# A new written-out order of all engines and loads for fused attention and a two-way maxout layer

## The chip, the cores and the metric

The kernel runs on one core of one Trainium2 chip. The metric is device time in microseconds for one execution; the median of three runs of the kernel before is 359.53 us (359.02, 359.53 and 360.0).

Engines are named as in the profile: PE is TensorE, PEld its weight loads, ACT is ScalarE, DVE is VectorE, POOL is GpSimd, SP is SyncE, which issues most of the DMAs.

## The reference

For 8 batches and 8 heads, with 1152 positions and 64 values per head, neighbouring query rows are averaged in pairs (576 pooled queries), scored against all 1152 keys, put through a softmax, and multiplied by the values. The 4608 resulting tokens of 512 values go through two weight matrices; the larger of the two results goes through a third:

```python
q_pool = q.reshape(B, H, S // 2, 2, D).mean(axis=3)
scores = scale * np.matmul(q_pool, k.transpose(0, 1, 3, 2))
attn = softmax(scores)                       # row maximum taken off first
x = matmul(attn, v).transpose(0, 2, 1, 3).reshape(B * 576, 512)
h1, h2 = x @ w1, x @ w2                      # (512, 1024) each
out = np.maximum(h1, h2) @ w_out             # (1024, 512), float32
```

## The kernel before, in words

**Attention.** Two heads of one batch form a pair; there are 32 pairs. For each pair q, k and v are loaded (0.59 MB each, three buffers for each kind), cast to bf16 by GpSimd (q is summed over its two rows at the same time), and q and k are transposed. For the first five pairs TensorE transposes (`qtrans`, `ktrans_pe`), for the others VectorE transposes q in eight steps (`qtrans_dve`, L446) and a transposing DMA does k (`ktrans`, L436). The scores of all pairs form one long row of 324 groups of 512 columns for both heads. A step `S` (`scores`, L290) computes a group on TensorE in two PSUM banks, with 64-row tiles, both heads at once; a step `E` (`exps`, L305) puts it through the exponential on ScalarE. No maximum is subtracted. Pair i begins in group 10.125 x i; pair 12 in group 121.

**Values.** For each pair and head four chunks of nine matmuls (`chunk`, L569, full 128-row tiles, only 65 columns each) multiply the exponentials with the values and a column of ones. The last 64 queries of two pairs are taken together (`rest`, L584, 18 matmuls each). VectorE divides by the sum; the result is transposed to `xT`, by TensorE (`xtrans_pe`, L660) for eight pairs and by DMA for the others.

**The maxout layer** uses max(h1, h2) = h2 + max(h1 - h2, 0). The difference `wd` of the two weights is formed once by GpSimd (`w_diff`, eight steps, in the order `W_DIFFS`), and the product `w21` of w2 and w_out once by TensorE (`w2t_job` and `w21_job`, L530 and L543). Then `h` jobs (L694) compute the difference for up to 512 tokens and two blocks of 128 features, `p` jobs (L737) the result for 256 tokens, from `xT` with `w21` and from the rectified differences with w_out. Three `z` jobs (L780) do the last 256 tokens. h and p use 64-row tiles, z full ones.

**The order.** Nothing is scheduled at run time. A long string names one step per character, and each character appends the next step of its kind to the program: `S` a score group, `E` an exponential, `A` a chunk or a rest, `0` to `3` one unit (two matmuls) of the h or p job that is open under that number, `4` to `9`, `+` and `-` the emptying of its banks by VectorE or ScalarE, `K`, `Q`, `T`, `W`, `X`, `Z`, `F` other TensorE work (transposes of k and q, of w2, the units of `w21`, transposes to `xT`, the final jobs, filler), `l` a load, `t` and `x` a transposing DMA, `o` and `z` a store, `k`, `q`, `v`, `d`, `e` the steps of GpSimd, `r` a transpose of q on VectorE, and so on. Each engine executes its own steps in the order of the string; `Plan.solve` puts a semaphore wait wherever a step needs what another engine wrote or still reads. `MOE` gives the order of h and p jobs, `BANKS` one digit per job or score group, the PSUM bank it takes, and `LOADS` the order of the loads. From exponential 40 on a load also waits for the exponential two before the latest one in the string (`pace`). The `cost=` numbers are left over from the planner that made the strings and do nothing at run time.

TensorE has 1541 steps with 6009 matmuls, and one weight load for each matmul.

Of the kernel before, what the change touches and what calls it, by code (L numbers as in the profile page):

```python
# [116 lines left out]
def bass_funnel_attn__then__act_maxout2_kernel(  # L117
# [45 lines left out]
    LOADS = (  # L163
# [14 lines left out]
    )  # L178
    MOE = (
        "hhhhpphhhhpphhhhhhhhpphhhhpphhhhphhhhpphhhhphhhhphhhhpphhhhhphhhhphhh"  # L180
    )
    BANKS = (
        "0102346702674670602456042760460245602456012456214624160246246021460234064032646203460426704064036206"
        "2402642604264206250624024624624620742064064060560640640240260246124064024026412640240240240240246246"
        "2562462464267024602462062402462562624640646246246246246206206036026206260202612602402614262642042040"
        "4040645064064062416240204620642642674264240246240634062062462074206406406065060460240240240240202404"
        "2064306426046060467046064060640265026404024024012640260420460142604206406406420101420002406206204232"
    )

    ctx = ExitStack()  # L190
    with ctx:
# [603 lines left out]
        def store_z(lo, c0, c1, o):  # L795
            todo = []
            for half in range(2):
# [91 lines left out]
                 "m": ("Z", 0), "4": ("0", 0), "5": ("1", 0), "6": ("2", 0), "7": ("3", 0),  # L889
                 "8": ("0", 1), "9": ("1", 1), "+": ("2", 1), "-": ("3", 1)}  # L890
        for c in (
            "lululllfyFKklQfgFbKSgklKEKgSgSEFlFSyFFEQblESkSSElKcKElgTEkgShSESlKyEgQlEKbvgSSESlScEAeAlAEcAAAEASlaa"
            "qAESaSaTlEcTSEAlhQqEhSTlEbXvShESjlQcESEAlESbAcAEAlASkSaEaWaSalWaEWaWcAESSlAcAEAKWlEdaSaWWgEWSldiSEXS"
            "jWEkWjlWWWEWqSSlEKWgWWeiEQlSbSEkWWSlEWWvtWWEWSiSvAEKAgKdEAgAlSaSaEqAAAEAlSaEaAEArSdlrSEArAArdESrSWrA"
            "EWrdAAalEAaaXaSdaAaESljWWaEdWaSrWlEWWkSi1E1SlXqtEjS1j1SEv1rS1r1E1reA5AEASlkAErS0a0aE0vt0rSSr0E0qSr00"
            "ErA4AqlAEASa1aE1Slr11xrES11r1kE1ErSA5AEtASrSEArAArESaSaAklaEAaaAaAESr0vl0a0aE0rSxS0rE00r11xr1E0rS114"
            "E1tS11E1rSe1r1E1SrSv1lE11S1Eq11l111ES1r1SElr1A5AEAAlSaSaoEArAoArEASr0q0Ea0a0Srx0ESr0kSr00ElrS0tr0v0E"
            "0rS0r0EArkArEAArSr0lE0S000ESAlAEAaSa0aE0alSaaAAEASal0akE0tXSj0eE1j14S11ESq11o1ESo11qr1E151S1E1Sl1rS1"
            "ErAvA5AlESAErSSlakAaEAtrAArE00Ea0aS0rxES0r00r0E1q4S11E1S1r1vEl1rS1SrEA5lAvEAArSSlErSArAEArAlaAaAEaSa"
            "1a1taE1Sa1a1vE1rSx1r1SEr1e1r1x1ESrS1r1E1qrS1rl1E1AAkEAAlSa1aE1SS1l1EAAAEAlSa1aE1tSr0E050E0Sx00E0rSSr"  # L900
            "0oE0rSo0r0oE0rAoArkEArAAAvSalSaEAaaAaAaEAlSav0a0E0S11110klE0111S10Et5010S1110ESe1111050E011114Sq1111"
            "ElXA5SoSqjESoAjrAAErAAaAalEAr0000Sa0a01E01lr0S1x4E1SrS1r1E1tr1005E00SE0E0rS0r0q1E14S1l1EAkrASrSlEvAr"
            "ArAEArAlaSa1EaSaAaAalAErSv1a1Ea10lrS0x5E0q0S00ESrx11kr0E0rS1t14Ee1S11E1rSS1rE1rAlArEAArS1aqaE1lS1S1E"
            "S11l1E11S1ErtAkArAEArSa1aE11rxS1r0E005S0E0S0ro0SEr0oS0ro0E0qoAAESAkAEAASav0aESaAaaAaAElASalv0aE0SXrt"
            "E0j0S0jrSE1e1r110rE1Sr11l1Er0S500E011lrS11ErS11q11ElA5AASSlEAAaAaEAASa0aE1k0xS411E1SE111t1rESA5AEvoA"
            "rSoSrEAArAEAr0aSa00alE0aSa0a00E0rSlA4AEA0vaSa0lE0rSxSr0k0E0r00rx0EqSr10r0E0trSe10rE0Sr01rE11Sq0E0l0S"
            "00E0S0l0E014S1E11l1SoSEAoAAokEAAaAaAASa1aE1tSrSE1r1E1rSx11rE1Sr11rE11rS1Er1A5qAEAASoSvESoAAAElaAkaAa"
            "AaEla00a0v0Sa00aE1111xS11rE111115100x111e4S01E0005St0000ErS0400E0Sr00rESl0r00r0E00rSlSrE0Sq000ESl000"
            "EAAlAEAAaAaAASaSakE0t0r00Er1E0r1xS14E1S111EroS1r1o1E151S1E1Sr1S1ErA5AvEAAArSklSESAlrAqAEtaaAaAa0aE0a"
            "Sv0a0aESrxSe0r0E01r0x1rE114S1E1S1l1rSE5AAAElASrSEaAaAlArEAqSa1a1E1lSSxr1E1Sr11rE1t1rSk1rE11Sr1E1r11r"  # L910
            "AEAvS1E1SAqlAEAlS1E1SAAlEaSaaAaAEaAaSka1aE1Sx1r1vSE0500x0E0eSr0SErAtArAEArSao0aE00orSSr0EArAAEqASla0"
            "aE0Sx11110E1111S50E00l1Sk11Er1tSE0r1111Er00S50E01r111Sr11E11rSl0500ES4AAEvASroSESroAAqlAEAaAaAaEAlaa"
            "0Sav00E0aSa000t0r1E1k41S1E1rxSe0r00E0rSx1r00E0rS1r01E14lS11E1rSS1lqE1AAEAAAaAaAASa0a0E00xS00E00S411t"
            "Ek11ESr00E0r0Sr10E0r00Sr1E14S111ErSA5AEvAASroSESroAAoAEaAoaAaAaEaSav111aE1a00xS0Er0S1r11xE1rSe0500E0"
            "tS0r0E0r0SrSE0rS0r00E0000E0SS0E00A4EAAAAaAoaAoASaSaE11x11SES11E1E11511E1S11ES11151E11S1E1S1S1EA5AvEA"
            "AAAAaAaAaAaaSaSE0a0a00xSES000E0x0400E0e00SSE00000E0SS0E0000ES0S0E0S00E00040E00S00EoS0oAEAoAAoAaAaAAA"
            "aAaAxAAAAaAaAaAaa0a100a0a30X0j3100j22221330223323020+130-111301313913000233330-2281122000o01111o2911"
            "0101003381133223311339222-2000222022110222330003382232233+221111o111o31-2o1123333222133233+111-11111"
            "111Z9ZZZZZoZZoZZZZZZmZZZZzzZZZZZZZZZZmZZZZZZZzZzmzz"
        ):  # L920
            step(c)
        plan.solve()
# [51 lines left out]
```

## Time and profile before

| what | value |
|---|---|
| median of three runs | 359.53 us |
| the profiled execution: its time, its span | 360.63 us, 358.9 us |
| granted TensorE clock | 1.00 |
| TensorE busy | 349.2 us, 97% |
| ScalarE busy | 315.3 us, 88% |
| VectorE, GpSimd busy | 236.0 us, 143.4 us |
| DMA | 84.67 MB, 236 GB/s on the mean |
| exponentials (L305) | 303.8 us in 336 instructions |

A busy TensorE says that some matmul was on its way, not that it ran at its peak: matmuls overlap, and most rows give one matmul's own duration, several times the distance from one start to the next. The distance between starts in the timeline is the cost of a step. "issue" as a releaser is time in which an engine waited for nothing that the profile shows. The queue "q8 instruction" brings instructions.

### The profile page before, as it was taken

Reading aid. Unit: us, or ns where it says so; the run is one execution under the profiler, and the core shown is the slowest. Engines: PE = TensorE matmul, PEld = TensorE weight load, DVE = VectorE, ACT = ScalarE, POOL = GpSimd, SP = SyncE. Lnnn points to the kernel's source line nnn. Section 1 sums busy time; section 2 is a strip of 40 time slices with the busy share of each in tenths; the row PEclk is TensorE's granted clock in tenths of the full one; section 3 lists DMA queues with packets and bytes.
Section 4 is the critical chain, followed back from the end, with each engine's and each line's share of the span. In section 5 each row is a group of like instructions: output and inputs, shape, how many; then the busy total and the mean of one; then the engine's idle time right before and its main releaser. Section 6 shows DMA issues by size and latency. Waiting matters only on the chain.

```text
span 358.9 us, 13458 instructions
## 1 busy us (share of the span) xinstructions
PE 349.2 (97%) x6009; PEld 218.0 (61%) x6009; DVE 236.0 (66%) x516; ACT 315.3 (88%) x355; POOL 143.4 (40%) x128
## 2 busy tenths in 40 slices
PE   7699999999999999999999999999999999999996
PEld 5465655655566675656664675666676655657663
DVE  3686578977798658976796776884787774514001
ACT  5999989999999989999999898999999898890431
POOL 2446997363645171744417152535425220100000
PEclk9999999999999999999999999999999999999999
DMA  8999999999999999998999989899999853002224
GB/s 264 409 392 395 316 374 257 298 244 291 314 244 315 288 294 297 329 260 148 343 209 301 233 217 305 187 274 255 196 265 228 170 113 75 17 23 59 60 60 117
DMA packets 77434, 84.67 MB, mean 236 GB/s; under 512 B 49216, under 2 KB 50496, under 8 KB 77376
## 3 DMA queue, kind: packets, MB, share of 16 engines
q1 hardware_dynamic: 76592, 83.28, 88.3%
q8 instruction: 47, 0.77, 0.9%
q10 hardware_dynamic: 784, 0.52, 0.5%
q14 instruction: 11, 0.09, 0.1%
HBM read 62.91 MB, written 9.44 MB: 202 GB/s over the span
## 4 chain that ended last, share of the span: by engine, by line
PE 92%; DMA 3%; ACT 2%; SPq 1%; issue 1%; DVE 0%
PE ps L737 25%; PE ps L290 21%; PE ps L569 21%; PE ps L694 18%; PE ps L584 3%; DMA qraw<-in_q_dram 3%; ACT et L305 2%; PE ps L543 2%; PE ps L780 1%; PE ps L660 1%; SPq L325 0%; PE ps L491 0%; PE ps L512 0%; SPq L336 0%; PE ps L663 0%
## 5 line engine op out<-in xcount | busy, mean ns | idle before, releaser
L305 ACT ACTIVATE et<-ps 128x1024 bf16<-128x1024 f32 (+1 forms) x336 | 303.8, 1016 | 14.0 <-PE ps L290 13.1
L290 PE MATMUL ps<-qpT,kT 64*128 64x256 bf16 (+7 forms) x1162 | 114.5, 283 | 1.2 <-DVE qpT L498 0.6
L446 DVE STREAM_TRANSPOSE qpT<-qp 32x288 bf16<-32x288 bf16 x216 | 101.4, 469 | 12.7 <-PE ps L290 6.0
L694 PE MATMUL ps<-xT,wd 64*128 64x512 bf16 (+3 forms) x832 | 84.1, 311 | 0.0
L569 PEld LDWEIGHTS ps<-vE,et 128*128 128x128 bf16 x2304 | 73.6, 97 | 16.9 <-issue 10.0
L569 PE MATMUL ps<-vE,et 128*128 128x65 bf16 x2304 | 81.5, 193 | 1.9 <-issue 1.4
L737 PE MATMUL ps<-wo,stage 64*128 64x512 bf16 x544 | 78.4, 376 | 0.0
L290 PEld LDWEIGHTS ps<-qpT,kT 64*128 64x128 bf16 x1162 | 47.6, 94 | 48.4 <-ACT et L305 15.1
L411 POOL TENSOR_TENSOR qp<-qraw 128x576 bf16<-128x576 f32 x30 | 42.1, 1406 | 53.8 <-DVE qpT L446 48.9
L417 POOL TENSOR_SCALAR vE<-vraw 128x1152 bf16<-128x1152 f32 x32 | 36.9, 1152 | 56.8 <-PE ps L584 39.3
L694 PEld LDWEIGHTS ps<-xT,wd 64*128 64x128 bf16 x832 | 36.0, 94 | 24.5 <-ACT et L305 1.7
L381 POOL TENSOR_SCALAR kbf<-kraw 128x1152 bf16<-128x1152 f32 x31 | 35.7, 1151 | 32.5 <-DMA kraw<-in_k_dram 24.6
L705 DVE TENSOR_SCALAR stage<-ps 128x1024 bf16<-128x1024 f32 (+3 forms) x40 | 39.1, 979 | 13.4 <-PE ps L694 12.7
L737 PE MATMUL ps<-w,xT 64*128 64x512 bf16 x272 | 39.9, 377 | 0.0
L737 PEld LDWEIGHTS ps<-wo,stage 64*128 64x128 bf16 x544 | 25.8, 94 | 18.5
L598 DVE RECIPROCAL rc<-ps 128x4 f32<-128x4 f32 (+1 forms) x64 | 11.8, 184 | 35.5 <-PE ps L569 34.9
L606 DVE TENSOR_TENSOR xnat<-ps,rc 128x256 bf16<-128x256 f32 x64 | 27.2, 424 | 1.9
L429 POOL TENSOR_SCALAR rem<-et 128x1152 bf16<-128x1152 bf16 x16 | 18.4, 1152 | 20.9 <-ACT et L305 20.8
L743 DVE COPY stage<-ps 128x1024 f32<-128x1024 f32 x14 | 17.0, 1216 | 11.6 <-PE ps L737 11.4
L709 ACT ACTIVATE stage<-ps 128x512 bf16<-128x512 f32 (+1 forms) x12 | 6.0, 525 | 17.4 <-PE ps L694 17.4
L785 DVE COPY stage<-ps 128x512 f32<-128x512 f32 (+1 forms) x2 | 1.0, 492 | 25.7 <-PE ps L780 25.7
L737 PEld LDWEIGHTS ps<-w,xT 64*128 64x128 bf16 x272 | 12.6, 94 | 8.5 <-ACT et L305 0.2
(46 smaller groups left out, 138.5 us busy)
## 6 DMA issues: line engine op xcount, KB each, us to landing
vraw<-in_v_dram SPq DMA_DIRECT2D x32, 576.0 KB, 6.1
kraw<-in_k_dram SPq DMA_DIRECT2D x31, 576.0 KB, 7.0
qraw<-in_q_dram SPq DMA_DIRECT2D x31, 576.0 KB, 6.2
out_dram<-stage SPq DMA_DIRECT2D x24, 256.0 KB, 3.8
out_dram<-stage SPq DMA_DIRECT2D x21, 128.0 KB, 3.0
xT<-in_moe_w_dram SPq DMA_DIRECT2D x4, 512.0 KB, 11.2
stage<-in_moe_w_out_dram SPq DMA_DIRECT2D x4, 512.0 KB, 13.6
stage<-in_moe_w_dram SPq DMA_DIRECT2D x4, 512.0 KB, 14.0
```

The source lines that it names most:

```text
L290: last = e.matmul(ps[:, h, col:col + hi - lo], kT[i % 3][rows(h), t, :], qpT[i % 3][rows(h), lo:hi], start=True, stop=True)
L305: op("ACT", lambda e: e.activation(et2[:, :, c:c + z - a], ps[:, :, a - g * W:z - g * W], EXP, scale=scale), r=[f"b{m}", f"b{m + 1}"], w=w ...
L381: op("POOL", lambda g: g.tensor_scalar(kbf[s][:, :, :, :].rearrange("p t h d -> p h t d"), kraw[r][:, :, :, :], 1.0, 1.0, ALU.mult, ALU.mu ...
L411: op("POOL", lambda g: g.tensor_tensor(qpf[s][:, :, :], qraw[r][:, :, 0, :], qraw[r][:, :, 1, :], ALU.add), r=[f"qraw{r}"], w=[f"qp{s}.0", ...
L417: op("POOL", lambda g: g.tensor_scalar(vE[r][:, :, :, 0:D].rearrange("p t h d -> p h t d"), vraw[r][:, :, :, :], 1.0, 1.0, ALU.mult, ALU.m ...
L429: op("POOL", lambda g: g.tensor_scalar(rem[:, :, :, :], src, 1.0, 1.0, ALU.mult, ALU.mult), r=[f"et{i % 2}.{g - first(i)}" for g in range( ...
L446: op("DVE", lambda e: e.transpose(view[dst:dst + 32, :, 32 * pb:32 * pb + 32], qpf[s][src:src + 32, :, 32 * db:32 * db + 32]), r=[f"qp{s}. ...
L569: last = e.matmul(fb[m][:, sb * 66:sb * 66 + 65], et[:, a:a + P], vE[vs][:, t, half, 0:65], start=(t == 0), stop=(t == NT - 1))
L606: todo.append(evac_op("DVE", lambda e, m: e.tensor_tensor(xnat[xs][:, i % NHP, :, half * D:half * D + D], a(m)[:, 0:NCH, 0:D], rc[half][:, ...
L694: last = e.matmul(fb[m + k][:, 0:size], wd[z, ct, (f0 + k) * P:(f0 + k + 1) * P], xT[z, ct, n0:n1], start=(turn == 0 and ct == 0), stop=(t ...
L705: return e.tensor_scalar_max(gT[:, f0:f0 + 2, g0:g0 + size], wide[m // 2][:, :, 0:size], 0.0)
L737: last = e.matmul(fb[m + k][:, :], lhs, rhs, start=(turn == 0 and j == 0), stop=(turn == 1 and j == NC_ + NF - 1))
```

## The change

The kernel's steps and formulas stay, and so do `MOE` and the numbers of loads, jobs and steps. Four strings and lists are replaced: `W_DIFFS` (the order of the eight `w_diff` steps), `LOADS` from its 20th entry to where it becomes regular near pair 17, `BANKS`, and the string of the order. A constant `FOUR = 1` is added that nothing reads. The two order strings have the same 2751 characters in another sequence. They differ most in the first 50 us, less in the middle, and again at the end, where the last h jobs and the last p job are interleaved in another way. The start of each changed part:

```diff
-    W_DIFFS = ((0, 0), (0, 1), (3, 1), (1, 1), (1, 0), (3, 0), (2, 1), (2, 0))
+    W_DIFFS = ((1, 1), (1, 0), (0, 0), (3, 0), (3, 1), (0, 1), (2, 1), (2, 0))
...
+    FOUR = 1
...
-        ("q", 2), ("w", 0, 3), ("q", 3), ("v", 1), ("w", 2, 0), ("w", 2, 1), ("k", 3), ("w", 2, 2),
-        ("w", 2, 3), ("w", 1, 0), ("k", 4), ("q", 4), ("k", 5), ("v", 2), ("v", 3), ("w", 1, 3),
-        ("q", 5), ("w", 1, 1), ("w", 1, 2), ("k", 6), ("q", 6), ("v", 4), ("k", 7), ("v", 5), ("q", 7),
-        ("q", 8), ("k", 8), ("k", 9), ("v", 6), ("v", 7), ("q", 9), ("q", 10), ("k", 10), ("v", 8),
-        ("k", 11), ("k", 12), ("q", 11), ("q", 12), ("k", 13), ("v", 9), ("q", 13), ("v", 10), ("v", 11),
-        ("v", 12), ("v", 13), ("q", 14), ("k", 14), ("v", 14), ("v", 15), ("k", 15), ("k", 16),
+        ("q", 2), ("w", 0, 3), ("q", 3), ("v", 1), ("w", 2, 0), ("w", 2, 1), ("w", 2, 2), ("w", 2, 3),
+        ("k", 3), ("v", 2), ("k", 4), ("q", 4), ("w", 1, 1), ("w", 1, 0), ("k", 5), ("v", 3), ("q", 5),
+        ("w", 1, 3), ("q", 6), ("w", 1, 2), ("k", 6), ("v", 4), ("q", 7), ("k", 7), ("q", 8), ("v", 5),
+        ("k", 8), ("q", 9), ("v", 6), ("q", 10), ("k", 9), ("k", 10), ("k", 11), ("v", 7), ("v", 8),
+        ("v", 9), ("v", 10), ("q", 11), ("v", 11), ("v", 12), ("q", 12), ("q", 13), ("v", 13), ("k", 12),
+        ("v", 14), ("k", 13), ("q", 14), ("k", 14), ("k", 15), ("q", 15), ("k", 16), ("q", 16),
...
-        "0102346702674670602456042760460245602456012456214624160246246021460234064032646203460426704064036206"
+        "0102346540241601204627067462062401627426402316403643064206340436204620432604260345624064206524062402"
...
-            "lululllfyFKklQfgFbKSgklKEKgSgSEFlFSyFFEQblESkSSElKcKElgTEkgShSESlKyEgQlEKbvgSSESlScEAeAlAEcAAAEASlaa"
-            "qAESaSaTlEcTSEAlhQqEhSTlEbXvShESjlQcESEAlESbAcAEAlASkSaEaWaSalWaEWaWcAESSlAcAEAKWlEdaSaWWgEWSldiSEXS"
-            "jWEkWjlWWWEWqSSlEKWgWWeiEQlSbSEkWWSlEWWvtWWEWSiSvAEKAgKdEAgAlSaSaEqAAAEAlSaEaAEArSdlrSEArAArdESrSWrA"
+            "lululllfyFKklFfgQFbFkSlKEKKggSgSlEFySFEQblkESSESlKcESlgTkEShKElgKySEgQlEKbvgSSESlScEAeAlAcEAATElaSaq"
+            "ThESAlhAEScAESlSqaTEaAhlQEvQbSblESScXESElAjAEcAAElSAaaESaSaaAlaAEcSAEWWlWkaWaEWScSlKEvKWgWEWlgSkiSE"
+            "WWWlESqWWKEWgWlSeSESAlWdEAiAAESaldSaAEQSbklAEAAESvataSWEWWqWWWEWWSidSlEKXrEAgEAdljSSjErAXrAdAEjArSSE"
...
```

More of the change, by code (lines that the diff above doesn't have):

```diff
@@ new lines, in bass_funnel_attn__then__act_maxout2_kernel @@
+            "SSE5AAAElArSSaEAaArlAAEr0E0aSa0lE0r1Sxr01Er1S0q0E014S1E1Sq11rSEA5AvEAArSSElSrkArAAErAlAaatAEaSav1a1a"
+            "E11aSa11ErxSeSr11Er11x1r1ESrS1r1E1r1lSr1kE1rAArAElArSta1aE1S1S1EAAAEASa1aE1lS50Ex0q0E0S0SEo00rk0o0Er"
+            "0oSr0o0ESrtArAEvrAArAArSSakEaAaAalAaEAaSav0a0El0S11110E01S11l10E50tS01111E0Se11110E50011114S1111qEXA"
+            "l5SSojESkAjorAAErAAaqAaEAr0000lSa0a001E1rxS01r1ES411r1ESrl1005tE00SE0E0rS0r01E14S11EAlrAvSrSEArAlrAE"
+            "ArAqaSa1EaSlaAaAaAErSv1la1Ea1Srx00E500kS0xE00rS1r0E1etS411E1S1qrSE1rAArEAkArlSa1aE11rS1r1lESS11E1Sl1"
@@ new lines, in bass_funnel_attn__then__act_maxout2_kernel @@
+            "1EAAAEAlSa1aE1t1rS1r1ESr1x01rE005qS0E0S0roAEkAroSr0oE0rSvo000ESlAAEAASla0aESaAaaAaAElASav0aE0SXlrE0j"
+            "tS00jrSE1e1r110rE1Srq111Er0S500lEk011rS11ErSl1111EqA5AAlSSEAAaAalEAASa0aE10xSk411E1SE111t1rESA5AEvoA"
+            "rSoSrEAArAEArSa0a0E0a0aSal0a0E00rSA4EAlASva0aE00rxS0r0kE0SSxr0E0q0r00rE0tSr1e0Er00Sr0E0r0Sr00E0qSl00"
+            "E0S411El1S11EoSAoAEAoAAaAaAlASaSaE11tr11kr1E1rSESx1rE1Sr11rE11rS1Er11Sl11E1Aq5AEAASovSESoAAAElaAaAaA"
+            "aEa00av00lSa00aE1111xSk11rE111115100x111e4S10E0005St0000ErS0400E0SrS0rE00r0l0r0E00rSSrE0lSq000ES00l0"
@@ new lines, in bass_funnel_attn__then__act_maxout2_kernel @@
+            "EAAAEAlAaAaAASa0akESt0r10Er0E0r1xS14E1S111EroS1r1o1E151S1E11rS1SErA5AvEAAArSklSESArtAqAEaaAaAa0aESa0"
+            "v0a0aESrxSe0r0E00r1x14E11S1E1lrS11rSE5AlAAEASrSElaAaAArEASa1la1E1xSSr1E1Srq1t1rE11r11rE1kSr11E1rSSr1"
+            "1ElAAvE1SAEAqlAS1E1SlAAEaSaaAaAElaAaSva1aE1Sx1r1SkE0500x0E0eSr0SErAtArAEArSao0aE00orS0rSEArAAEqASa0a"
+            "E0lS111x10E1111S50E010Sk10lEr11EStr011Er110S50E01r111Sr11E11rS050l0ES4AAEvASroSESroAAqAElAaAaAaEAaa0"
+            "0alv00Sa1aE0000xS41k1E1Sr00xEr00e1rS00rE0t00r0004S1E000rS1rE11rSl11Eq10S41E1l1S1SEAAAEAAaAaAASa0a0E0"
```

45 lines of the change are left out of this document (16 added, 29 removed), and 12 rows, old and new, of the table LOADS.

## The prediction

> **What bounds the kernel now.** I read the page first, then the waits, the windows and the timeline. Busy shares, slices and the chain of the kernel before:
>
> ```profile
> span 358.9 us, 13458 instructions
> PE 349.2 (97%) x6009; PEld 218.0 (61%) x6009; DVE 236.0 (66%) x516; ACT 315.3 (88%) x355; POOL 143.4 (40%) x128
> ...
> PE   7699999999999999999999999999999999999996
> ...
> ACT  5999989999999989999999898999999898890431
> ...
> PE 92%; DMA 3%; ACT 2%; SPq 1%; issue 1%; DVE 0%
> ```
>
> TensorE carries 92% of the chain and is idle for 358.9 - 349.2 = 9.7 us. The changed kernel has the same 1541 TensorE steps and 6009 matmuls, so it can win only idle time, or the cost of one step following another. How the other engine that matters, ScalarE, stands beside it, by stage (columns: stretch, its length, busy and instructions of PE, PEld, DVE, ACT, POOL, then clock, DMA share, GB/s):
>
> ```profile
> 0.00:15.00 15.00, 11.04 (x155) 7.95 (x155) 6.80 (x16) 10.79 (x13) 4.10 (x13) 1.00 0.90 322
> 15.00:47.00 32.00, 30.80 (x577) 19.51 (x575) 23.15 (x47) 31.88 (x37) 22.42 (x19) 1.00 1.08 368
> 49.00:118.00 69.00, 69.00 (x1157) 40.92 (x1155) 56.60 (x126) 67.75 (x76) 38.87 (x33) 1.00 1.11 285
> 118.00:322.00 204.00, 203.48 (x3578) 126.61 (x3576) 143.42 (x310) 192.49 (x214) 76.02 (x63) 1.00 0.90 220
> ```
>
> Four stages. To 15 us TensorE lacks 4.0 us, with DMA at 0.90. From 15 to 118 us both engines are full: ScalarE lacks 0.1 us in the first part and 1.25 us in the second. From 118 us only TensorE is full; ScalarE lacks 11.5 us. Soon after 322 us ScalarE has no exponentials left. The waits of the whole run (us, times, longest) and the two long holes on TensorE:
>
> ```profile
> PEld ps L290 <- ACT et L305: 15.1, 61, 0.4
> ...
> ACT et L305 <- PE ps L290: 13.1, 20, 1.8
> ...
> PEld ps L569 <- issue: 10.0, 37, 1.2
> ...
> PE ps L569 <- issue: 1.4, 2, 0.9
> ```
> ```profile
> 46.92 0.39 PE L543 MATMUL ps<-wo,xT 128*128 128x512 bf16 x1
> 48.19 0.43 PE L569 MATMUL ps<-vE,et 128*128 128x65 bf16 x9 [0.87 <-issue]
> ```
> ```profile
> 135.34 0.76 PE L569 MATMUL ps<-vE,et 128*128 128x65 bf16 x20
> 136.62 0.77 PE L569 MATMUL ps<-vE,et 128*128 128x65 bf16 x20 [0.52 <-issue]
> ```
>
> "issue" means that no semaphore or DMA explains the hole. Most of the 37 on PEld are about 0.2 us, before a change of tile form, which is costed below; two such waits are on PE itself. Where do they fall in the instruction stream?
>
> ```profile
> 0.00:46.93 46.93, 41.77 (x729) 27.39 (x729) 29.89 (x61) 42.60 (x49) 26.45 (x32) 1.00 1.02 353
> 42.10:46.93 4.83, 4.83 (x129) 3.55 (x125) 3.49 (x10) 4.80 (x7) 4.69 (x5) 1.00 1.33 199
> ...
> 0.00:136.10 136.10, 130.07 (x2259) 81.23 (x2260) 99.04 (x218) 129.45 (x145) 75.80 (x72) 1.00 1.07 310
> 129.45:136.10 6.65, 6.65 (x130) 4.43 (x125) 3.79 (x9) 6.24 (x8) 4.84 (x4) 1.00 1.19 266
> ```
> ```profile
> q8 instruction: 47, 0.77, 0.9%
> ```
>
> 729 and 2259 matmuls stand ahead of the holes: 1530 between them, with as many weight loads 3060 instructions. Queue 8 moved 0.77 MB in 47 packets, 16.4 KB each; 0.77 MB over 12,018 matmuls and loads is 64 bytes an instruction, so a packet is some 256 of them, and 3060 is twelve packets less about one wait instruction in each. Both holes lie on a packet's edge: TensorE had run out of fetched instructions.
>
> **The change, part by part.**
>
> *The fetch at 48 us.* The single L543 matmul at 46.92 should take 0.22 us (six of them take 1.40 us in the chain below), and the next starts 1.27 us later: the hole costs 1.05 us. The packet ahead of it (128 matmuls) began near 42.0 us and ran dry in 4.9 us, while the next packet was there only 6.2 us after that start. In the new order I count matmuls 602 to 729: 46 in L569 against 67, 8 in L543 against 1, 14 transposes against none, the rest equal. An L569 matmul costs 0.030 us (20 from 135.34 to about 135.95), a transpose some 0.06 (four, with a change of tile form, from 328.21 to 328.54).
>
> ```profile
> 34.03 1.40 PE ps L543 x6
> ```
> ```profile
> 328.21 0.40 PE L660 MATMUL ps<-ident,xnat 128*128 128x128 bf16 x4
> 328.54 0.20 PE L663 MATMUL ps<-ident,xend 64*128 64x64 bf16 x1
> ```
>
> So the packet lasts 4.9 - 21 x 0.030 + 7 x 0.22 + 14 x 0.06 = 6.6 us, over the 6.2. At 136 us the packet began at 129.3 and its successor came 7.3 us later. With 6.2 nothing is left of the hole, with 7.3 still 0.7. I take 6.2, the nearer in place and traffic: **-1.05**, ends -0.35 and -1.05. ScalarE gains it too, since its hole there is as long:
>
> ```profile
> 45.41 3.78 ACT L305 ACTIVATE et<-ps 128x1024 bf16<-128x1024 f32 x4
> 50.24 3.88 ACT L305 ACTIVATE et<-ps 128x1024 bf16<-128x1024 f32 x4 [1.05 <-PE ps L290]
> ```
>
> The Trainium skill speaks against this term. Its page "Runtime: NRT & Kernel Launch", section "Instruction fetch mechanics", has the sequencer fetch the next 16 KiB block of 256 instructions while it runs the current one, and calls the cost of a boundary "mostly hidden". The trace agrees on the block's size, and on most of its 47 edges; on two it doesn't. By the rule alone this term and the next would be 0.
>
> *The fetch at 136 us.* Twenty L569 matmuls from 135.34 end near 135.95; the hole to 136.62 is 0.67 us. The 128 matmuls ahead are the same in the new order (18 of p, 40 of h, 24 scores, 6 transposes, 40 of L569), so it is filled only if the packet comes sooner. The loads in front differ: v15 is moved from after exponential 117 to after 134, and k16 from after 120 to after 129, behind q15. That packets can come in time for shorter stretches, two windows show:
>
> ```profile
> 65.00:70.00 5.00, 5.00 (x125) 3.71 (x120) 4.75 (x14) 5.00 (x7) 2.05 (x2) 1.00 1.19 244
> ...
> 124.60:129.30 4.70, 4.70 (x136) 3.83 (x132) 3.06 (x10) 4.05 (x5) 3.13 (x4) 1.00 0.88 219
> ```
>
> Packets of 5 us there cost no hole. Between -0.67 (gone) and +0.67 (twice as long), with one or two loads fewer queued in front: **-0.3**.
>
> *Changes of tile form.* Two h pairs followed by scores take 0.44 us, two followed by L569 0.53 us:
>
> ```profile
> 59.54 0.59 PE L694 MATMUL ps<-xT,wd 64*128 64x512 bf16 x4
> 59.98 0.38 PE L290 MATMUL ps<-qpT,kT 64*128 64x256 bf16 x4
> 60.19 0.59 PE L694 MATMUL ps<-xT,wd 64*128 64x512 bf16 x4
> 60.72 0.75 PE L569 MATMUL ps<-vE,et 128*128 128x65 bf16 x19
> ```
>
> 0.09 us for going from 64-row tiles to the full array. Counted in the two order strings, the old one has 203 neighbours of unlike tiles, the new one 199: 4 x 0.09 = 0.36 at most. All four are saved by the score step 92, near 93 us, where ScalarE paces and TensorE would only wait longer for it. I take **-0.1**, ends -0.36 and 0.
>
> *Score steps placed earlier.* In the ScalarE-paced stage the new order puts some score steps ahead of other work, S96 by 1.8 us, onto a bank that exponential 93 frees, S94 by 0.5. The bank can't be free sooner, since ScalarE has no slack. Other such waits are at most 0.4 us each (the first waits row). While ScalarE paces they cost nothing at the end; as far as it doesn't, they add. **+0.15**, ends 0 and +0.8.
>
> *Start and loads.* The first 19 loads keep their order, and with them the 4.0 us that TensorE lacks. Then the four loads of w_out go together, two of them now ahead of k3, and three of w1 behind k4 and q4. k3's row:
>
> ```profile
> L325 SPq DMA_DIRECT2D kraw<-in_k_dram x1: 4710/4710/4710, 11.6 to 11.6; - x1
> ...
> DMA to landing us min/median/max: 15.8/15.8/15.8
> ```
>
> It lands at 27.4; two 0.52 MB loads at 398 GB/s (the next row) put it at 30.0, its cast (L381, 1.15 us) ends at 31.2, and by equal TensorE work its transposes come at 31.5. Cost 0, cover 0.3 us; without the cover TensorE waits that much longer, behind it the scores of pair 3. GpSimd's w_diff steps follow the arrival of w1 and end at about the same place. 0, ends -0.3 and +0.5.
>
> ```profile
> 15.00:25.00 10.00, 8.83 (x197) 6.37 (x194) 8.38 (x15) 9.91 (x12) 6.27 (x5) 1.00 1.03 398
> ```
>
> *SyncE's queue from 60 to 160 us.* SyncE issues in order, so a load that waits for its ring holds every transposing DMA and store behind it. k9 is issued ten exponentials later, q9 eleven earlier; v9 to v14 come six to eleven earlier, k12 to k16 two to twenty later. The v loads need the cast three pairs back: v12 after exponential 96 has it after 91, v13 after 100 has it after 93, so none should hold the queue. GpSimd's casts (L381, L411, L417) move with their loads; it is busy 38.87 of 69.0 us in that stage and has room. VectorE's eight L446 transposes for each pair end within some 3 us of where they did; pair 9's end six earlier. I cost all this at nothing: the cover is the 2.8 us of pair 12, the tightest, in the third rival.
>
> *Tail.* TensorE has as much work, the last feed-forward jobs are closed in another order, and the three final jobs with their stores are the same: 0. `FOUR` is read nowhere.
>
> Sum: -1.05 - 0.3 - 0.1 + 0.15 = -1.3 us. The profiled execution took 360.63 us, its span and 1.73 us around it: 359.3. The median shown, 359.53, lies 1.1 lower: **358.2**.
>
> **The rivals.**
>
> *Fetch waits only move* (the change doesn't do what it says). Edges stay where the count puts them, and the traffic of the reordered loads delays other packets: for it, one packet at 129 us needed 7.3 us; against it, the 6.6 us packet above. The first two terms fall away: 359.53 - 0.1 + 0.15 = 359.6. The skill's rule of hidden fetches ends there too.
>
> *All of it is won.* Both holes (1.72), all four changes of form (0.36) and 0.3 at the start: 357.1. For it, TensorE has nothing else that waits after 118 us; against it, ScalarE's pace before.
>
> *K of pair 12 is late*: slower. Its load is moved from after exponential 82 to after 101, its transposing DMA from 100 to 109, and the first scores of pair 12 (S121) stay behind 120.
>
> ```profile
> 99.77 18.81 ACT L305 ACTIVATE et<-ps 128x1024 bf16<-128x1024 f32 x21
> ```
> The k loads between 60 and 125 us, then the kT transposes between 100 and 125, then all k loads:
> ```profile
> DMA to landing us min/median/max: 4.6/6.2/7.6
> ```
> ```profile
> DMA to landing us min/median/max: 6.3/6.8/7.4
> ```
> ```profile
> DMA to landing us min/median/max: 3.5/6.8/15.8
> ```
>
> 19 exponentials at 18.81/21 = 0.90 us are 17.0 us; 6.2 + 1.15 + 6.8 = 14.2 are needed, so 2.8 us are spare. It decides from a landing of about 9 us on, and gives "slower" from some 11.5. At 12.5 us, 3.5 are missing: 358.2 + 3.5 = 361.7. Against it, 7.6 is the longest near there; for it, the 15.8, when loads were queued deep.
>
> **How the numbers follow.** No change to the measurement is about 0.3%, 1.1 us: faster is below 358.45, slower above 360.6. The forecast, 45%: its own range is 357.6 to 359.0; two thirds of it are faster (30%), a third the same (15%). Fetch waits move, 22%: the same 19%, slower 3% with a new hole of 1 us and more. All won, 17%, faster. K late, 16%, slower. Together faster 47%, same 34%, slower 19%. The range leaves out half of K late and the lowest part of "all won": 357.0 to 360.2.
>
> **What would show it.** Near matmul 729 TensorE has no issue hole over 0.4 us; ScalarE's 1.05 us hole is gone and exponential 50 starts about 1 us sooner. At matmul 2259 the hole is shorter, or not. From 49 to 118 us ScalarE has under 0.3 us idle. Wrong: an issue hole on another packet's edge; L290 waiting for a kT transpose near 119 us; TensorE idle over 5 us before 25 us; ScalarE idle in the middle with TensorE waiting for a bank.

## The result, and the profile after

The changed kernel takes 361.38 us (median of 18 runs, 360.59 to 365.52), the kernel before 359.70 beside it (358.86 to 362.36). The ratio is 1.0047 with a 95% interval of 1.0027 to 1.0067: 1.7 us slower, 3.2 above the forecast and above its range. Run again unaltered it took 361.36 (12 runs; 361.14 without the two of them that are over 1.5% above the fastest). There are two traces of it: the first execution took 360.83 us, with a span of 359.1, the second (after_again) 363.40, with a span of 361.6. In the changed file every line number is one higher than before: L291 scores, L306 exponentials, L570 AV, L695 and L738 the feed-forward steps.

The busy row and the slices of TensorE and of its granted clock, first trace:

```profile
PE 350.9 (98%) x6004; PEld 219.8 (61%) x6009; DVE 236.8 (66%) x517; ACT 315.2 (88%) x354; POOL 143.3 (40%) x128
...
PE   7899999999999999999999999999999999999996
...
PEclk9699999999999999999999999999999999999999
```

Against before, one more instruction runs on VectorE and one fewer on ScalarE: the two order strings have the same length but not quite the same characters (`7` stands once where before has none, `+` five times for three, `-` twice for five), and with that VectorE empties one bank that ScalarE emptied. It lies at the end, which the halves below find to cost nothing.

The first trace has one slice at a lower clock (last section); the second has none. So the second is the cleaner one to set beside before. Its stages, in the columns of the prediction's table:

```profile
0.00:15.00 15.00, 11.47 (x155) 7.87 (x155) 6.84 (x16) 10.60 (x13) 4.75 (x14) 1.00 0.90 327
15.00:47.00 32.00, 30.16 (x571) 19.53 (x575) 22.25 (x45) 31.70 (x37) 21.23 (x18) 1.00 1.06 373
49.00:118.00 69.00, 67.82 (x1122) 40.33 (x1121) 56.22 (x124) 68.06 (x76) 36.79 (x31) 1.00 1.04 275
118.00:322.00 204.00, 201.33 (x3546) 126.44 (x3544) 142.71 (x310) 189.13 (x210) 78.65 (x65) 1.00 0.93 222
```

TensorE lacks 1.8 us between 15 and 47 us, where before lacked 1.2, then 1.2 between 49 and 118, where before lacked nothing, and 2.7 between 118 and 322, where before lacked 0.5. What it waited for, in the waits of the second trace, has no semaphore and no DMA behind it:

```profile
PEld ps L695 <- issue: 2.1, 1, 2.1
PE ps L695 <- issue: 2.0, 2, 1.7
...
PE ps L291 <- issue: 0.7, 1, 0.7
```

In TensorE's timeline these are a hole at 70 us and one at 188 us (second trace). A third, as long as the first, stands at 150 us; the view gives it to a VectorE transpose, but the next section shows that it ends as the others do:

```profile
69.33 0.31 PE L291 MATMUL ps<-qpT,kT 64*128 64x320 bf16 x2
70.33 0.26 PE L291 MATMUL ps<-qpT,kT 64*128 64x192 bf16 x2 [0.69 <-issue]
...
150.16 1.04 PE L695 MATMUL ps<-xT,wd 64*128 64x512 bf16 x8 [0.63 <-DVE qpT L447]
...
188.87 0.34 PE L695 MATMUL ps<-xT,wd 64*128 64x384 bf16 x2 [1.71 <-issue]
```

All three stand at the edge of a 256-instruction packet, and so does a smaller one at 181.2 us (0.47). The first trace has the one at 188 us too, smaller:

```profile
186.13 0.34 PE L695 MATMUL ps<-xT,wd 64*128 64x384 bf16 x2 [0.29 <-issue]
```

The two holes of before are gone. First trace of the changed kernel, where before had its hole of 1.05 us, and second trace, where before had 0.67 us:

```profile
47.34 0.98 PE L570 MATMUL ps<-vE,et 128*128 128x65 bf16 x27
48.24 0.61 PE L291 MATMUL ps<-qpT,kT 64*128 64x512 bf16 x4
48.78 1.26 PE L570 MATMUL ps<-vE,et 128*128 128x65 bf16 x36
```
```profile
135.43 1.74 PE L570 MATMUL ps<-vE,et 128*128 128x65 bf16 x52
```

So the first two steps of the forecast came true in the trace (the packet ahead of the edge at 48 us lasts 6.7 us, forecast 6.6), and ScalarE lacks 0.27 us between 49 and 118 us in the first trace, as forecast (0.94 in the second). The time went the other way, and of the signs named for a wrong forecast the first has come: an issue hole on another packet's edge.

### The profile page after: what moved, and what is told of

Read it like the earlier page. It is cut to its first block, busy times and chain, and to the rows that moved or that the text cites. A ratio compares the mean times of both kernels' runs of the same rounds, so it can differ in the third digit from the quotient of the medians.

```text
span 359.1 us, 13461 instructions
## 1 busy us (share of the span) xinstructions
PE 350.9 (98%) x6004; PEld 219.8 (61%) x6009; DVE 236.8 (66%) x517; ACT 315.2 (88%) x354; POOL 143.3 (40%) x128
## 4 chain that ended last, share of the span: by engine, by line
PE 86%; ACT 9%; DMA 2%; DVE 1%; SPq 1%; issue 0%
PE ps L738 25%; PE ps L570 19%; PE ps L291 19%; PE ps L695 18%; ACT et L306 9%; PE ps L585 3%; DMA xT<-in_moe_w_dram 2%; PE ps L781 1%; PE ps L544 1%; SPq L326 0%; DVE stage L744 0%; DVE xT L455 0%; PE ps L661 0%; PE ps L513 0%; PE ps L531 0%
## 5 line engine op out<-in xcount | busy, mean ns | idle before, releaser
L306 ACT ACTIVATE et<-ps 128x1024 bf16<-128x1024 f32 (+1 forms) x336 | 304.1, 1010 | 15.5 <-PE ps L291 14.3
L291 PE MATMUL ps<-qpT,kT 64*128 64x256 bf16 (+7 forms) x1162 | 116.3, 286 | 1.0 <-DVE qpT L499 0.7
L695 PE MATMUL ps<-xT,wd 64*128 64x512 bf16 (+3 forms) x832 | 84.0, 311 | 0.5 <-issue 0.3
L570 PEld LDWEIGHTS ps<-vE,et 128*128 128x128 bf16 x2304 | 73.4, 97 | 15.2 <-issue 7.4
L570 PE MATMUL ps<-vE,et 128*128 128x65 bf16 x2304 | 81.4, 193 | 0.1
L738 PE MATMUL ps<-wo,stage 64*128 64x512 bf16 x544 | 79.1, 376 | 0.0
L291 PEld LDWEIGHTS ps<-qpT,kT 64*128 64x128 bf16 x1162 | 48.1, 94 | 50.4 <-ACT et L306 13.9
L706 DVE TENSOR_SCALAR stage<-ps 128x1024 bf16<-128x1024 f32 (+3 forms) x41 | 39.9, 973 | 36.0 <-PE ps L695 35.6
L695 PEld LDWEIGHTS ps<-xT,wd 64*128 64x128 bf16 x832 | 35.6, 94 | 24.5 <-PE ps L695 1.4
L738 PE MATMUL ps<-w,xT 64*128 64x512 bf16 x272 | 40.0, 376 | 0.0
L738 PEld LDWEIGHTS ps<-wo,stage 64*128 64x128 bf16 x544 | 25.6, 94 | 18.1
L738 PEld LDWEIGHTS ps<-w,xT 64*128 64x128 bf16 x272 | 12.7, 94 | 9.2
L603 DVE TENSOR_TENSOR xend<-ps,rc 64x64 bf16<-64x64 f32 x64 | 14.2, 221 | 1.2
```

The costliest lines, as they stand in the source:

```text
L291: last = e.matmul(ps[:, h, col:col + hi - lo], kT[i % 3][rows(h), t, :], qpT[i % 3][rows(h), lo:hi], start=True, stop=True)
L306: op("ACT", lambda e: e.activation(et2[:, :, c:c + z - a], ps[:, :, a - g * W:z - g * W], EXP, scale=scale), r=[f"b{m}", f"b{m + 1}"], w=w ...
L570: last = e.matmul(fb[m][:, sb * 66:sb * 66 + 65], et[:, a:a + P], vE[vs][:, t, half, 0:65], start=(t == 0), stop=(t == NT - 1))
L695: last = e.matmul(fb[m + k][:, 0:size], wd[z, ct, (f0 + k) * P:(f0 + k + 1) * P], xT[z, ct, n0:n1], start=(turn == 0 and ct == 0), stop=(t ...
L706: return e.tensor_scalar_max(gT[:, f0:f0 + 2, g0:g0 + size], wide[m // 2][:, :, 0:size], 0.0)
L738: last = e.matmul(fb[m + k][:, :], lhs, rhs, start=(turn == 0 and j == 0), stop=(turn == 1 and j == NC_ + NF - 1))
```

## What the traces say about packets

The trace has a start for each of the 47 packets on queue 8. I call "late" the time from the edge at which TensorE enters one packet (its weight load) to the start of the transfer of the next, and "hole" what TensorE lacks at the next edge, over the 0.213 us of a usual step. In eleven traces, at five edges (named by the time of the edge in the kernel before; late / hole, us):

```
order at the edge, kernel                42         64         129        144        180
before    before, first trace            3.8/1.04   1.8/0      5.1/0.50   2.9/0      0.8/0.17
before    before_again                   2.9/0.21   1.7/0      4.9/0.36   3.4/0.10   0.9/0.17
before    tail_after_192                 2.9/0.21   1.8/0      5.1/0.57   3.3/0.12   0.8/0.17
changed   changed, first trace           2.1/0      2.9/0      2.6/0      2.9/0.01   3.8/0.56
changed   after_again                    2.8/0      3.7/0.78   2.5/0      3.6/0.79   4.6/1.97
12 moved  after_12_letters               2.8/0      4.0/0.62   3.1/0      4.1/1.18   1.4/0
50 moved  after_50_loads                 2.8/0      3.6/0.64   5.0/0.05   2.8/0.02   1.5/0
51 moved  after_51_loads                 3.0/0      4.1/0.83   4.6/0      3.2/0.36   1.7/0
2 moved   before_2_letters               2.9/0.24   1.9/0      1.4/0      3.1/0      1.0/0.17
few bytes few_bytes_before               2.4/0.21   1.0/0      0.4/0      0.7/0      0.9/0.17
few bytes few_bytes_after                1.3/0      1.2/0      1.1/0      0.9/0.01   1.0/0
```

The 0.17 at 180 stands in before's order even with few bytes, so it is no fetch wait. The 0.21 at 42 isn't one either: it is the step from scores to the L543 matmul, two matmuls ahead of the edge, 0.43 us in every trace of that order. At the edge itself the step is 0.22 us with few bytes and in before_to_92, 1.26 in the first trace of before and 0.39 to 0.45 in before_again, tail_after_192 and before_2_letters; so the fetch costs 1.04 us there in one execution and 0 to 0.23 in the others.

The traces also show what ends a hole. In the eleven traces and the other four of the halves below, TensorE crosses 675 edges, and it never starts on a packet less than 1.23 us after the end of that packet's transfer. At the edges behind the first 30 us it has 23 holes over 0.35 us; 22 of them end 1.31 to 1.60 us after the end of the transfer, those at 150 us among them (1.33 to 1.49). The exception is one in before_to_92 at 187 us, which ends 2.48 us after. The transfer itself takes 0.9 to 1.2 us in these cases, and 2.3 for the hole of 1.97 us. So a packet is there some 2.5 us after its transfer starts, and a stretch leaves a hole where it is shorter than the lateness and these 2.5 us together. The stretches between edges last 5.2 us (42, in before's order), 5.4 (64), 6.6 (129), 5.3 (144) and 5.7 (180) without a hole; in the 5.4 and 5.3 us stretches of the table every packet that starts 3.2 us late or more leaves one (0.10 to 1.18), and none that starts 3.1 or less does (0.02 at most).

## The experiments

**The changed kernel and the kernel before once more.** No edit.

> The changed kernel once more, unaltered, for a second trace of it. Its first trace holds a stretch from 11.42 to 18.25 us at half the granted clock, and exponential 10 started 1.38 us later than before there. Theory CLOCK: that stretch is the loss; a trace without it has exponential 44 within 0.3 us of before and a span of 357.5 to 358.2. Theory LOADS: the loss is in transfers that are issued later (k 12 to 16, v 7 to 14), and a trace at full clock still has a span of 359 to 360.5, with TensorE idle on SyncE or GpSimd work between 49 and 200 us. Theory TAIL: exponential 270 within 0.3 us of before and the last one 1.2 to 1.7 us later.

> The kernel before once more, unaltered, for a second trace of it. Theory FETCH, with waits that differ from one execution to the next: the 1.04 us of TensorE at 48.2 us in the first trace is gone or under 0.4 here, other packet edges have holes, and the span less the holes over 0.4 us at edges is 356.5 within 0.4 of the first trace's. Theory ORDER, and my prediction, which took the hole at 48.2 us for a fixed cost of this order: it stands there again, 0.9 to 1.1 us.

after_again took 361.36 us (ratio 1.0032, interval 1.0003 to 1.0060), the profiled execution 363.40, at full clock: theory CLOCK falls. Theory LOADS gave a span of up to 360.5 us, below the 361.6, and its cause doesn't show: the long waits are on no SyncE or GpSimd work. Exponential 44 starts 0.56 us later than before, exponential 186 1.16 and exponential 192 2.83 later, behind the hole of 1.97 us; TAIL falls too as the place of that loss. before_again took 360.25 us beside 359.89 (ratio 1.0009, interval 0.9982 to 1.0036). Its timeline, around 48 us and at 136:

```profile
46.89 0.61 PE L290 MATMUL ps<-qpT,kT 64*128 64x512 bf16 x4
47.43 0.39 PE L543 MATMUL ps<-wo,xT 128*128 128x512 bf16 x1
47.86 0.43 PE L569 MATMUL ps<-vE,et 128*128 128x65 bf16 x9
48.13 0.38 PE L543 MATMUL ps<-wo,xT 128*128 128x512 bf16 x1
...
135.43 0.34 PE L569 MATMUL ps<-vE,et 128*128 128x65 bf16 x6
136.15 0.83 PE L569 MATMUL ps<-vE,et 128*128 128x65 bf16 x22 [0.38 <-issue]
```

From the L543 matmul to the next instruction it is 0.43 us here, against 1.27 in the prediction's rows. The hole at 48 us is a matter of the execution, the one at 136 us of this order: it is in all four traces that have it at that time (0.57 in head_after_48). One number of the expectation missed: the span less the holes over 0.4 us is 358.2 - 0.7 = 357.5, not 356.5.

**Halves joined at 48, 92 and 192 us.** The order string, the banks and the loads of one kernel up to a letter at which both have done the same work, and those of the other behind it (banks renamed so that those in use at the seam agree).

```diff
-order = changed[:2751]
+order = before[:287] + changed[287:]        # head_before_48
+order = changed[:287] + before[287:]        # head_after_48
+order = changed[:624] + before[624:]        # after_to_92
+order = before[:624] + changed[624:]        # before_to_92
+order = before[:1399] + changed[1399:]      # tail_after_192
```

> The other half: the changed order up to score step 44, then the order of before. Theory CLOCK or a slower start: 360.8 to 361.4, the loss stays. Theory LOADS or TAIL: 358.3 to 359.0, which is before less the fetch hole of 1.05 us at 48 us, if the new start itself costs nothing.

> The order of before up to score step 44 (its first 287 letters, the loads and weight differences that go with them), then the changed order from there on. Theory CLOCK or a slower start: the time is that of before or less, 359.2 to 359.8, since all of the loss was in the first 48 us. Theory LOADS: no gain from the swap, 361.0 to 361.6 plus what the fetch hole at 48 us costs if it comes back (1.05), so 361.4 to 362.4. Theory TAIL: the same as LOADS.

> The order of before up to score step 185 (1399 letters, 82 of the loads), then the changed order. Theory TAIL: 360.9 to 361.4, most of the loss. Theory CLOCK and theory LOADS: 359.5 to 359.9, the time of before, since the start and the loads between 48 and 190 us are those of before.

> The order of before to score step 88, then the changed one. Theory EDGE-180: 360.8 to 361.6, most of the loss. Theory EDGE-64: 359.7 to 360.4.

> The changed order to score step 88 (624 letters, 92 us, 48 of the loads), then that of before. Theory EDGE-180 (the fetch waits that tell the two apart lie behind 92 us, at the edge at 180 us above all): 359.4 to 360.2. Theory EDGE-64 (they lie at the edge at 64 us, where the second trace of the changed kernel has 0.78): 360.6 to 361.4.

- tail_after_192: 360.07 us, ratio 1.0002 (0.9971 to 1.0034). The tail behind 192 us costs nothing that can be told.
- head_after_48: 360.68, 1.0018 (0.9994 to 1.0041). This is the forecast's first step alone: the hole at 48 us is away, and the kernel is not faster. It lies between the two ranges expected; its trace has holes of 0.57 at 136 us and 0.73 at 150, so it doesn't price the step by itself.
- before_to_92: 361.54, 1.0049 (1.0023 to 1.0075), as slow as the changed kernel, with holes of 0.74 and 0.78 us at 150 and 187 us (the second is the exception named above). Most of the loss can arise behind 92 us.
- head_before_48: 362.93, 1.0095 (1.0070 to 1.0121), and after_to_92: 365.88, 1.0125 (1.0074 to 1.0176). Both brought waits of their own at the seam, so their times don't place the loss. TensorE's timeline, the first around 55 us, the second at 101 us:

```profile
53.60 0.59 PE L695 MATMUL ps<-xT,wd 64*128 64x512 bf16 x4
55.12 0.39 PE L695 MATMUL ps<-xT,wd 64*128 64x512 bf16 x2 [0.93 <-POOL wd L465]
```
```profile
100.85 0.39 PE L291 MATMUL ps<-qpT,kT 64*128 64x512 bf16 x2 [2.91 <-DVE stage L706]
```

**Few bytes.** Every instruction of TensorE, ScalarE, VectorE and GpSimd stays; the loads of q, k and v carry one ninth of their bytes from pair 6 on.

```diff
 def load_k(i, lo=0, hi=NT, eng="SP"):
+    full, hi = hi - lo == NT, 1 if i >= 6 else hi
 ...
-    vraw[s][:, :, :, :]
+    vraw[s][:, :, 0:hi, :]
```

> The changed kernel, with the loads of q, k and v cut to one ninth of their bytes from pair 6 on (the rest of each buffer keeps what an earlier pair left, so the output is not the reference's; every instruction of the four engines stays). From some 50 us on the DMA engines are then mostly free. Theory FETCH: no packet starts more than 1 us after it is asked for, no hole over 0.4 us at a packet's edge after 60 us, 358.0 to 359.0. Theory ORDER: 360.5 to 361.4.

> The kernel before with the same cut. Theory FETCH: 357.6 to 358.6, and the two cut kernels stand 0.2 to 0.7 us apart, what is left of 1.7 once the fetch waits are gone. Theory ORDER: the two stand 1.4 to 1.9 us apart, as with all bytes.

The changed order takes 359.20 us (ratio to the kernel before 0.9984, 0.9965 to 1.0004), the order of before 359.00 (0.9974, 0.9954 to 0.9993; 12 runs each): by the medians 0.2 us apart instead of 1.7. The changed kernel has lost 2.2 us, the one before 0.7. Both stand a little above what theory FETCH gave (358.0 to 359.0 and 357.6 to 358.6); the distance is what it gave. Stages of the changed order with few bytes (busy of PE, clock, DMA share, GB/s):

```profile
49.00:118.00 69.00, 68.67 (x1145) 1.00 0.45 92
118.00:200.00 82.00, 82.00 (x1478) 1.00 0.44 98
```

The same windows of after_again, with all bytes:

```profile
49.00:118.00 69.00, 67.82 (x1122) 1.00 1.04 275
118.00:200.00 82.00, 79.33 (x1396) 1.00 1.10 265
```

At the five edges the packets start at most 1.3 us late (2.7 at one of the longer stretches) and TensorE has no hole over 0.01 us. Fewer bytes also free GpSimd from waits for loads. That these don't account for the difference follows from TensorE's other holes: over 0.43 us and away from packet edges, between 30 and 352 us, they sum to 9.4 and 9.9 us in the two traces of the changed kernel and to 9.6 with few bytes (before: 9.2 and 9.5, and 9.2). Theory ORDER falls: by the medians, 1.5 of the 1.7 us need the bytes.

**Which loads.** In the first, twelve letters "l" (SyncE's next load) are moved to where before has them (since a letter is whatever load comes next, q 16 and v 15 go out earlier too); in the second the last 51 loads, of which the list calls the 60th and on; in the third v 6 as well.

```diff
-letters of loads 65 to 76 at 1030 ... 1263 (q 20), 1270 (k 20)
+                       at  957 ... 1194 (q 20), 1203 (k 20)      # after_12_letters
+letters and list of loads 60 to 110 as before                   # after_50_loads
+the same, and the letter of v 6: 436 -> 417                      # after_51_loads
```

> The changed kernel, with only twelve letters of its string moved: the loads 65 to 76 (v 16 to k 20, whose order is the same in both kernels) stand at the places of before, 26 to 73 letters earlier; SyncE then hands out q 20 and k 20 near 157 us and not in a burst of four at 167 to 169 us. Theory FETCH: the packet asked for at the edge at 180 us starts within 1.5 us, the hole at its end is under 0.3 us where the two traces of the changed kernel have 0.56 and 1.97, and the time falls to 360.0 to 361.0. Theory ORDER: 361.1 to 361.6.

> The changed kernel with its last 51 loads (from the 60th on, some 125 us) in the order and at the places of before. Theory FETCH, if the places of these loads are what makes the packets late: 359.7 to 360.7, with the holes at 150 and 186 us as in the traces of before (0.1 to 0.7 and 0.17). If only some edge is always late whatever the places, as moving twelve letters gave (the hole of 186 us gone, one of 1.18 at 150): 361.1 to 361.7.

> The kernel with the last 51 loads of before in the changed order, and one letter more: v 6 goes out where before has it, near 61.5 us, and not 1.2 us ahead of the packet edge at 64 us. Theory FETCH: the packet of that edge starts within 2.5 us (3.6 before), the hole of 0.64 at 70 us is under 0.25, and the time falls from 360.6 to 359.7 to 360.3, so that the change is left with little more than the 0.2 us that it stood behind with few bytes. If only the median of a spread moves: 360.3 to 360.8.

after_12_letters: 361.69 us (1.0045, 1.0018 to 1.0071), no gain. Yet the place it aimed at came right. TensorE's timeline there, and at 150 us:

```profile
185.84 0.64 PE L570 MATMUL ps<-vE,et 128*128 128x65 bf16 x16
186.41 0.39 PE L291 MATMUL ps<-qpT,kT 64*128 64x448 bf16 x4
186.64 0.81 PE L695 MATMUL ps<-xT,wd 64*128 64x384 bf16 x8
```
```profile
149.53 0.38 PE L291 MATMUL ps<-qpT,kT 64*128 64x384 bf16 x4
150.93 0.60 PE L695 MATMUL ps<-xT,wd 64*128 64x512 bf16 x4 [1.02 <-DVE qpT L447]
```

The packet asked for at 180 us starts 1.4 us late where it was 3.8 and 4.6, and the hole is gone; the packet at the edge at 144 us is now 4.1 us late, with a hole of 1.18. (The view names a VectorE transpose as releaser there; the hole ends 1.39 us after the packet's transfer, as the others do.) No load goes out in the 6 us ahead of that edge. SyncE is busy with one transposing DMA from 140.9 to 145.9 us, five loads follow, and until the packet starts at 148.5 us most of what moves is packets of 256 bytes, those of the transposing DMA.

after_50_loads: 360.59 us (1.0034, 1.0019 to 1.0049), 0.8 below the changed kernel. The holes at 150 and 186 us are gone; that of 70 us, 0.64, is left. But the changed kernel's own second set has a ratio of 1.0032, so the 0.8 isn't settled. after_51_loads: 361.55 us (1.0044, 1.0018 to 1.0069), a miss. The letter moved, but v 6 went out at 62.0 us and not at 61.5: SyncE was handing out a transposing DMA from 60.7. Its packet still started 4.1 us late, and the hole was 0.83. It tested nothing but that a place in the string is not a time.

Two more kernels were to swap the loads from the 47th on, in both directions.

```diff
+LOADS and letters from the 47th load: those of before    # after_loads_before
+LOADS and letters from the 47th load: those of changed   # before_loads_after
```

> The changed kernel, with only its loads put back: from the 47th load on (v 9 and later, some 90 us to the end) the loads stand in the order and at the places in the string where before has them; the order of every engine's work is the changed one. Theory FETCH (the loss is TensorE waiting for instruction packets that wait in the DMA queues behind the changed loads, as at 188.9 us in the second trace of the changed kernel, 1.97 us, and at 186.1 in the first, 0.56): 359.9 to 360.5, the packet of the edge at 180 us starts within 1.5 us of being asked for instead of 3.8 to 4.6, and the hole at its end falls to the 0.17 us of before. Theory ORDER (the loss is in TensorE's own order, whatever the loads): 361.1 to 361.6, no change.

> The mirror: the kernel before, with the changed kernel's loads from the 47th on, in its order and places. Theory FETCH: 360.4 to 361.2, and the packet asked for at 180 us starts 3 us or more late, with a hole of 0.4 to 2 us at its end. Theory ORDER: 359.5 to 359.9, the time of before.

They took 366.43 and 367.13 us and say nothing: in the one the load of v 10 came to stand behind its own cast, in the other q 12, 19, 20 and k 12, 13, 20 did and two v loads came ahead of the cast three pairs earlier. So the casts worked on another pair's data, and the loads waited for the casts. The idea, changed loads alone in the kernel before, was not tried in a sound form.

**Fewer loads under way.** Each load of q, k or v from the 27th on waits on SyncE for the landing of the one before it, or the one before that.

```diff
+def behind():
+    seen[0] += 1
+    return [f"ld{seen[0] - 1}"] if seen[0] > 26 else []      # 2 for two loads
-    after=pace(), w=[f"vraw{s}"],
+    after=pace() + behind(), w=[f"vraw{s}", f"ld{seen[0]}"],
```

> The changed kernel, with one wait added on SyncE: from the 27th load of q, k or v on, each waits until the one before it has landed, so one is under way at a time (the bytes and every engine's order are unchanged). Theory FETCH: packets start within 2 us of being asked for at the edges at 64, 144, 180 us (3.8 to 4.6 in the traces of the changed kernel), the holes there are under 0.3 us, and the time is 359.2 to 360.4, the 359.2 of the kernel with few bytes at best. Theory ORDER: 361.1 to 361.6. If the wait starves the loads, TensorE waits for a kT or a qpT and the time is over 362.

> The same with two loads under way at a time. Theory FETCH: packets start at most 3 us late, holes in sum under 1 us, 359.6 to 360.8, between the changed kernel and the one with one load. Theory ORDER: 361.1 to 361.6.

> The kernel before with the wait for one load under way at a time. Theory FETCH: 359.0 to 359.7, at most the 0.7 us gained that the cut of the bytes gave, and the two kernels then 0 to 0.7 us apart. Theory ORDER: 1.4 to 1.9 us apart.

455.09, 373.58 and 456.53 us: the loads starve, and the times answer nothing. The packets in the traces answer something: over the same 29 edges (the 6th to the 34th) they start 0.7 us late on the mean in after_one_load and 0.6 in before_one_load, with no hole from fetching over 0.35 us, and 2.1 with two loads, as late as in the changed kernel and in before (2.1 to 2.2 in both traces of each; 0.5 and 0.4 with few bytes). The loads' bytes are all there, so it is the number of loads under way, rather than their bytes in all, that goes with late packets; the longer run, with DMA less busy (share 0.70 between 49 and 300 us), may have its part in it. The load row of the changed kernel with one at a time (loads, size, median us to landing), and its waits:

```profile
kraw<-in_k_dram SPq DMA_DIRECT2D x31, 576.0 KB, 4.2
```
```profile
POOL qp L417 <- DMA qraw<-in_q_dram: 105.7, 24, 11.6
ACT et L306 <- PE ps L291: 91.5, 49, 16.9
```

A load takes 4.2 us to land even when it has the engines nearly to itself; three for each pair are 12.6 us, more than the 10 us or so that a pair lasts (32 pairs, exponentials up to some 322 us), without the stores and transposing DMAs that wait behind them on SyncE.

**Two loads moved in the kernel before.** The other way round: cure the hole that all traces of before's order share.

```diff
-letters of q 16 and v 16 at 941 and 957
+                         at 986 and 994      # before_2_letters
```

> The kernel before, with two letters moved: q 16 and v 16, handed out 1.3 and 0.7 us ahead of the packet edge at 129.3 us, go out behind it (27 to 45 letters later). Theory FETCH: that packet starts within 3 us of being asked for and not 5.1, the hole at 136 us (0.50, 0.57 and 0.36 in three traces that have this order) is under 0.2, and the time is 359.2 to 359.7, 0.0 to 0.5 below before, at the bound of what can be told. If the loads' places do not matter: the hole stays at 0.4 to 0.6.

359.00 us (358.48 to 360.51, 12 runs) against 359.68: ratio 0.9979, interval 0.9961 to 0.9996, a little below the time expected. It is faster than both kernels, though the interval ends close to 1. TensorE at the place of the hole at 136 us:

```profile
134.43 1.61 PE L571 MATMUL ps<-vE,et 128*128 128x65 bf16 x48
```

q 16 and v 16 go out at 131.2 and 131.8 us, behind the edge at 128.2; the packet asked for there starts 1.4 us late and not 4.9 to 5.1, and the hole is 0. The gain of 0.7 us is a little over the 0.36 to 0.57 of the hole. This is the experiment that shows the mechanism best: no instruction of an engine's work is moved, only two loads, and the packet is early and the hole goes.

## Why the prediction was wrong

The step that failed is the first. **The fetch at 48 us, -1.05**, "ends -0.35 and -1.05": the hole is gone, as forecast, but it was no cost of this order. In before_again, tail_after_192, before_to_92 and before_2_letters, all with before's order there, the step at the edge is 0 to 0.23 us longer than with few bytes (0.60 in head_before_48, whose order changes at this place). It is worth near 0 in most executions, and head_after_48, which has this step, was not faster. The warning stood in the sum: "the median shown, 359.53, lies 1.1 lower" than the profiled execution's 360.63. That 1.1 is about the size of the hole, which no other trace of this order has. I took it off a second time.

**SyncE's queue from 60 to 160 us, 0** was the term that was mis-sized: I looked for a late k or v and priced the cover of pair 12. That cover held. No K of pair 12 was late (in the second trace its transposing DMA lands at 116.7 us and no matmul waits for it near 119), so the rival with 361.7 us came near the time with the wrong mechanism. What the moved loads did was to make packets late: with the bytes gone, 1.5 of the 1.7 us go. Put together, the forecast had the fetch waits fall by 1.35 us (-1.05 and -0.3), and by the few-byte kernels they rose by 1.5; all other terms were forecast at +0.05 and come to +0.2. So nearly the whole miss is in fetch waits: holes taken off that most executions don't have, and new ones priced at nothing.

**Fetch waits only move** was the right rival, and its price was wrong: 359.6 us assumed that they move at no cost, with 3% for more. The changed kernel has them at 70, 150 and 186 to 189 us, up to 1.97 us each, in stretches of 5.3 to 5.7 us. The packets aren't later on the mean than in before (2.1 to 2.2 us in all four traces), so the waits did move, to edges with short stretches ahead of them. Its medians lie 2.2 us above few bytes, those of before 0.7.

**The fetch at 136 us, -0.3**: right in sign. The hole is 0.36 to 0.57 in four traces of before's order and 0 in both of the changed kernel.

**Changes of tile form, score steps, tail** (-0.1, +0.15, 0): with few bytes the two orders stand 0.2 us apart, so these and the start together are worth +0.2, by medians, against a sum of +0.05. tail_after_192 bears out the tail.

**Start and loads, 0** with ends -0.3 and +0.5: k 3 was cast at 30.4 us (forecast 30.0) and its transposes began at 31.71 in after_again with 0.34 us of wait; in the first trace none waited. Within its ends.

**The Trainium skill**, page "Runtime: NRT & Kernel Launch", section "Instruction fetch mechanics", calls the cost of a boundary "mostly hidden". For the edge at 48 us it was nearer than my sum; at the edges at 64, 144 and 180 us it doesn't hold, where TensorE lost up to 1.97 us.

## What to carry to other kernels

Before a hole of one trace is priced, set the profiled execution's time beside the median: where it is slower by about the hole, the hole is in that execution and not in the kernel. When DMA is full, loads under way at a packet edge in TensorE's stream can delay the next 256 instructions. Between 45 and 190 us, in the thirteen traces with all bytes, the packet starts 0.8 us late on the mean with no load of q, k or v under way at the edge (14 edges), 1.9 with one (41), 2.2 with two (106), 3.0 with three (64) and 3.6 with four (26). How many of them were handed out in the last 1.5 us makes little difference (2.3, 2.7 and 2.3 us for none, one and two), and the scatter is wide: three are under way at 129 us in before and in the changed kernel, 5.1 and 2.6 us late. So look for short stretches, here those under the lateness and 2.5 us, and for how much is still under way at their edges. Moving a load clears one edge and may load another, so the whole queue has to be read, and a place in an order string is not the time of issue.

## What the runs showed that I had not expected

Queue 8's packets start up to 5.2 us after the edge with all bytes (at 150 us, in the first trace of before), and by 1.3 us at most at the same edges of the changed order with few. So small a transfer (16 KB) waits while others go on, and hardly waits when the loads have few bytes. But what moves meanwhile isn't always a load: in the first trace of before, while the packet of the 1.04 us hole waited from 42 to 45.7 us, most of the DMA time went to packets of 256 bytes, those of a transposing DMA issued at 38.7 us that took 9.2 us to land. How the engines share the queues no run shows.

In the first trace of the changed kernel the granted clock fell to about half for 6.9 us (stretch, length, busy of PE, clock, DMA share, GB/s):

```profile
4.00:11.40 7.40, 5.58 (x81) 1.00 1.04 383
11.40:18.30 6.90, 6.30 (x69) 0.51 1.03 409
18.30:25.00 6.70, 6.70 (x170) 1.00 1.04 392
```

TensorE was busy 5.58 of 7.40 us ahead of it, hardly less than before's 5.67, and exponential 10 started 1.38 us later than before's. The Trainium skill's page "TensorE: Matmul & The Clock Gate", part 1, gives half the clock after an idle window of a free-running monitor, some 3.4 us long; the half clock agrees, and that it came in one execution and not in the next fits a window that runs free of the kernel. An idle stretch of that length the trace doesn't show: TensorE's longest hole ahead of the half clock, from 4 us on, is 1.03 us. It isn't the cause of the loss: 15 of the 18 executions had a mean granted clock of 0.999 or more, and their median is 361.45 us.
